# Attention and two MLPs on one core: q loaded in 256-byte runs without an on-chip copy, its scale with one operand, and another instruction order

## The chip, the cores and the metric

The kernel runs on one core of one Trainium2 chip. The metric is the device time of one execution in microseconds (us). TensorE multiplies matrices (PE in the views; PEld is its weight load), VectorE (DVE), ScalarE (ACT) and GpSimd (POOL) work element by element, and SyncE (SP) issues all DMAs from one queue, in order.

## What is computed

The reference, cut to what matters (B, H, S, D = 4, 8, 576, 64):

```python
scores = np.matmul(q, k.transpose(0, 1, 3, 2)) / np.sqrt(D)
scores = np.where((rel >= 0) & (rel < 128), scores - slope[h] * abs(rel), -1e9)   # rel = query - key
attn = np.exp(scores - scores.max(-1, keepdims=True))
attn = attn / (attn.sum(-1, keepdims=True) + 1e-9)
x = np.matmul(attn, v).transpose(0, 2, 1, 3).reshape(2304, 512)
h = x @ w_in                                                                      # 512 x 2048
g = (a[0] + a[1]*h + a[2]*h**2 + a[3]*h**3) / (1 + abs(b[0])*abs(h) + abs(b[1])*h**2 + 1e-6)
x = g @ w_out
g = np.maximum(x @ w2_in, 0) ** 2
return g @ w2_out
```

All data are float32 in memory.

## The kernel before

The attention takes its 32 heads as 16 pairs p (four pairs to a batch), the two heads of a pair on the two halves of the 128 partitions. The first 512 rows of a pair are four tiles of 128 queries; the last 64 rows of each batch are loaded and transposed on their own (`load_rem`, `tr_rem`). One pair goes through these steps:

- **Load.** `load_qk` issues two DMAs for q and two for k (one per head), `load_v` two for v. For pair 0, and for v always, row t*128+p of a head goes to partition p, so that each run of memory is one row of 64 numbers, 256 bytes. For q and k of pairs 1 to 15, rows 4p to 4p+3 go to partition p (L379): each run is 1 KB, in a tile `qw` or `kw` laid out head, row, column.
- **Mix** (plan steps `iq`, `ik`; pairs 1 to 15). `mix` copies such a tile into `qr` or `kr`, laid out row, head, column, so that a row of both heads lies together. POOL, ACT or DVE may do it.
- **Transpose** (`trq`, `trk`). `tr_main` transposes four 128x128 blocks on TensorE into one PSUM bank. Where rows were loaded four to a partition, the destination is strided by 4, which puts the columns back in order.
- **Copy** (`trqc`, `trkc`). `tr_copy` takes the bank to SBUF (`qkT`). For q it also multiplies by `qs`, one number per partition: ACT uses the function Identity with two operands that hold one number per partition, the scale `qs` and a bias tile `zero` of zeros (L433); DVE uses a multiplication (L435). k's copy is plain (L350 on ACT, L352 on DVE).
- **Scores and softmax.** `s_pe` (L449, L458) multiplies; on DVE `join_keys` (L473) and `ttr` (L483) add the bias and find the row minima of the negated scores; `exp` runs on ACT (L498); `pt_pe` transposes the exponentials on TensorE (L533, L538, L543); `pt_copy` takes them to SBUF as `ptsb` (two of five tiles on DVE at L553, the others a plain copy on ACT or DVE); `pv_pe` multiplies by v (L576 to L589); `x_copy` takes the result to SBUF as `xT`, and DMAs write it to DRAM. The sums' reciprocals go through TensorE (`r_tr`, L513), are copied as `rt` (`r_copy`), written to DRAM, and later multiplied into x.

Beside the pairs, the weights of the first MLP are loaded (512 KB a chunk, L207) and split into a high and a low half: `wb`, then `win1hi` (a plain rounding copy) and `win1lo` (a difference), on ACT, DVE and POOL. At about 140 us the matmuls of the MLPs begin (L836, L923, later L987), and from 160 us on there is nothing else on TensorE.

The order is made by the class `Plan`: each step is added with the engines that may do it and a cost on each, with the steps that it waits for, and a priority. `run` repeatedly picks the step and engine that can begin first by these costs, plus a correction from the table `HOLD` (by step kind and engine), ties broken by priority, to which the table `BIAS` adds a number by step kind. The result is a fixed program for each engine and for SP's queue; every engine runs its instructions strictly in that order. The tables hold 99 and 84 numbers.

What the change touches: `load_qk` (L362), `tr_main` (L409), `tr_copy` (L425), the tile `zero`, the plan entries of q's and k's loads, mixes, transposes and copies (L620 to L664), and both tables.

Of the kernel before, what the change touches and what calls it, by code (L numbers as in the profile page):

```python
# [1400 lines left out]
```

## Time and profile before

| | |
|---|---|
| median of 3 runs | 919.96 us (917.84 to 920.03) |
| the profiled execution's own time | 919.47 us |
| its span, first to last instruction | 917.7 us |
| TensorE busy | 897.5 us of the span |
| VectorE, ScalarE, GpSimd busy | 659.5, 523.9, 433.7 us |
| TensorE's granted clock, mean | 0.998 of full speed |
| read from and written to DRAM | 102.76 and 31.01 MB |

An engine's busy time is the union of its instructions; what is left of a stretch is idle time, in which it waited. The DMA share is the mean busy share of the core's 16 DMA engines. A matmul's end is modelled, so short waits can hide inside a busy TensorE. In the rows below the attention is cut at the starts of the L449 matmuls of pairs 4, 9 and 15 (49.12, 91.92 and 137.40 us), so the second stretch holds five pairs and the third six.

### The profile page before, as it was taken

How to read it: one execution, taken by the hardware profiler on the slowest of the kernel's cores; microseconds unless marked ns; L12 is line 12 of the kernel's file. 1: busy time of each engine (PE TensorE's matmuls, PEld its weight loads, DVE VectorE, ACT ScalarE, POOL GpSimd, SP SyncE). 2: the span in 40 equal slices, each digit the busy share in tenths (PEclk: the TensorE clock that was granted, in tenths of full speed). 3: DMA queues.
4: the chain of work that ended last, by engine and by line, in shares of the span. 5: the costliest groups of instructions: out<-in, count | busy, mean ns of one | idle time of the engine just before them, and what ended most of it. 6: DMA issues, size and time to landing. Idle time of an engine off the chain costs nothing.

```text
span 917.7 us, 14434 instructions
## 1 busy us (share of the span) xinstructions
PE 897.5 (98%) x4748; PEld 736.2 (80%) x4748; DVE 659.5 (72%) x1310; ACT 523.9 (57%) x1157; POOL 433.7 (47%) x457
## 2 busy tenths in 40 slices
PE   7988999999999999999999999999999999999998
PEld 6666666888998888888888888888888888888896
DVE  5999988988889887888789787876554534455422
ACT  4988887877788777767777763332322211121232
POOL 4476545777457777686858864421550200000100
PEclk9999999999999999999999999999999999999999
DMA  8799853321323542453252558554523634782010
GB/s 187 237 278 284 216 167 110 110 74 47 94 70 122 179 136 93 136 186 116 103 172 104 181 187 281 182 194 126 171 92 93 210 110 138 213 314 91 2 46 23
DMA packets 114443, 134.73 MB, mean 147 GB/s; under 512 B 37424, under 2 KB 76736, under 8 KB 114368
## 3 DMA queue, kind: packets, MB, share of 16 engines
q1 hardware_dynamic: 114368, 133.81, 46.8%
q8 instruction: 37, 0.61, 0.3%
q14 instruction: 38, 0.31, 0.1%
HBM read 102.76 MB, written 31.01 MB: 146 GB/s over the span
## 4 chain that ended last, share of the span: by engine, by line
PE 87%; ACT 4%; DVE 3%; DMA 2%; POOL 2%; issue 1%; SPq 0%; POOLq 0%; DVEq 0%
PE y L923 41%; PE h L836 23%; PE ps L987 16%; PE o L576 2%; PE s L458 2%; ACT e L498 2%; DMA xrraw<-ys 1%; PE warm L748 1%; PE tr L414 1%; PE pt L543 1%; DVE e L483 1%; DMA ys<-yt 1%; PE pt L533 1%; DMA kw<-in_k_dram 1%; ACT xT L350 1%
## 5 line engine op out<-in xcount | busy, mean ns | idle before, releaser
L987 PE MATMUL ps<-xh,wc 128*128 128x512 f32 x448 | 148.8, 389 | 0.3 <-ACT ah L350 0.3
L836 PE MATMUL h<-xh,win1hi 128*128 128x512 f32 (+1 forms) x320 | 118.1, 369 | 0.2 <-DVE gl L243 0.2
L923 PE MATMUL y<-gl,wout1hi 128*128 128x512 f32 (+1 forms) x320 | 117.7, 368 | 0.0
L836 PE MATMUL h<-xh,win1lo 128*128 128x512 f32 (+1 forms) x320 | 117.7, 368 | 0.0
L923 PE MATMUL y<-gh,wout1hi 128*128 128x512 f32 (+1 forms) x320 | 117.7, 368 | 0.0
L836 PE MATMUL h<-xl,win1hi 128*128 128x512 f32 (+1 forms) x320 | 117.7, 368 | 0.0
L923 PE MATMUL y<-gh,wout1lo 128*128 128x512 f32 (+1 forms) x320 | 117.7, 368 | 0.0
L865 POOL TENSOR_TENSOR t<-t,ah 128x512 f32<-128x512 f32 (+1 forms) x80 | 97.3, 1217 | 37.4 <-ACT t L860 31.6
L923 PE MATMUL y<-wout2hi,gh 128*128 128x512 f32 x288 | 112.1, 389 | 0.0
L923 PE MATMUL y<-wout2hi,gl 128*128 128x512 f32 x288 | 112.1, 389 | 0.0
L923 PE MATMUL y<-wout2lo,gh 128*128 128x512 f32 x288 | 112.0, 389 | 0.0
L236 ACT ACTIVATE gh<-ah 128x512 fp32r<-128x512 f32 x64 | 40.3, 629 | 109.8 <-DVE ah L1019 109.8
L987 PEld LDWEIGHTS ps<-xh,wc 128*128 128x128 f32 x448 | 84.1, 188 | 18.2 <-ACT ah L350 0.7
L987 PE MATMUL ps<-xl,wc 128*128 128x512 f32 x224 | 87.1, 389 | 0.0
L243 DVE TENSOR_TENSOR gl<-h,gh 128x512 fp32r<-128x512 f32 (+1 forms) x96 | 57.5, 599 | 39.3 <-ACT gh L236 38.3
L243 POOL TENSOR_TENSOR xl<-xr,xh 128x512 fp32r<-128x512 f32 (+1 forms) x18 | 20.1, 1128 | 129.6 <-ACT xh L236 129.3
L236 ACT ACTIVATE gh<-h 128x512 fp32r<-128x512 f32 (+1 forms) x96 | 50.3, 524 | 44.1 <-PE y L923 39.1
L243 DVE TENSOR_TENSOR gl<-ah,gh 128x512 fp32r<-128x512 f32 x64 | 49.3, 772 | 35.6 <-ACT gh L236 35.4
L836 PEld LDWEIGHTS h<-xh,win1hi 128*128 128x128 f32 x320 | 60.3, 188 | 10.7 <-DVE gl L243 0.6
L849 ACT ACTIVATE ah<-h 128x512 f32<-128x512 f32 (+1 forms) x80 | 44.2, 553 | 42.6 <-PE h L836 41.9
L923 PEld LDWEIGHTS y<-gh,wout1hi 128*128 128x128 f32 x320 | 60.4, 189 | 10.0
L836 PEld LDWEIGHTS h<-xl,win1hi 128*128 128x128 f32 x320 | 60.3, 189 | 10.0
(161 smaller groups left out, 2125.3 us busy)
## 6 DMA issues: line engine op xcount, KB each, us to landing
wc<-wsum SPq DMA_DIRECT2D x64, 256.0 KB, 3.9
wc<-wp SPq DMA_DIRECT2D x48, 256.0 KB, 3.6
win1r<-in_moe_w_in_dram SPq DMA_DIRECT2D x16, 512.0 KB, 5.1
wout1r<-in_moe_w_out_dram SPq DMA_DIRECT2D x16, 512.0 KB, 3.7
win2r<-in_moe_w_in_dram SPq DMA_DIRECT2D x16, 512.0 KB, 4.0
wout2r<-in_moe_w_out_dram SPq DMA_DIRECT2D x16, 512.0 KB, 4.7
xrraw<-ys SPq DMA_DIRECT2D x44, 128.0 KB, 4.0
xs<-xT SPq DMA_DIRECT2D x16, 288.0 KB, 4.5
```

The lines of the kernel that those rows point to most:

```text
L236: nc.scalar.activation(dst, src, AF.Copy)
L243: (nc.vector if eng == "DVE" else nc.gpsimd).tensor_tensor(dst, a, b, ALU.subtract)
L350: nc.scalar.activation(dst, src, AF.Copy)
L414: nc.tensor.transpose(dst, st[p]["qk"[n]][:, t].rearrange("p h d -> p (h d)"), ident)
L458: nc.tensor.matmul(ps[j][:, i % 2, :w], qT[js, qs_], kT[js, k0:k1], start=True, stop=True)
L498: nc.scalar.activation(e, e, AF.Exp, scale=-1.0, bias=s[:, j : j + 1], accum_out=sums[p % 3][:, c : c + 1],)
L576: nc.tensor.matmul(st[p]["o"][rows[j], kb * P : kb * P + w], vr[:, kb, j, :], pt[:, j, 2 * kb * P : 2 * kb * P + w], start=(i == 1), stop= ...
L836: nc.tensor.matmul(h[:, :n], a[:, c * P : (c + 1) * P], bb[:, :n], start=(m == 0), stop=(m == 3 * NCC - 1),)
L849: nc.scalar.activation(gt("ah", 2, ji, f), tl["h", ji, f], AF.Abs)
L865: nc.gpsimd.tensor_tensor(tl["t", ji, f], tl["t", ji, f], tl["ah", ji, f], ALU.mult)
L923: nc.tensor.matmul(dst, a, bb, start=(first and m == 0), stop=(last and m == 2))
L987: nc.tensor.matmul(dst, w, x, start=(k in (1, 2, 5) and m == 0), stop=(m == 5), skip_group_check=True)
```

## The change

Of q and k, only k (`LONG = 'k'`) keeps the 1 KB runs and the copy. q of every pair is loaded in 256-byte runs straight into `qr`, the tile that is transposed, and has no `qw` and no mix. Its load therefore waits for the transpose of q two pairs earlier (there are two `qr` tiles) and no longer for the mix two pairs earlier, and its transpose waits for the load itself. The number of DMAs stays; those of q have four times as many runs. On ACT, q's scale becomes the function Copy with the scale operand alone; `zero` goes. The costs of some steps are set anew, and both tables are replaced, so every engine's program is another. In the new program, ACT does all 17 scalings.

```diff
@@ the tables: 99 and 84 numbers replaced by 99 and 83
-BIAS = {'js': -354.3, 'm1': -417.1,
+BIAS = {'js': 653.6, 'm1': -2152.6,
...
@@ in the kernel
     MERGED = (2, 3)
+    LONG = 'k'
...
-    zero = acst.tile([P, 1], F32, name="zero")
...
-    nc.vector.memset(zero, 0.0)
...
         if t0 == 0:
-            if p == 0:
+            if p == 0 or nme not in LONG:
                 st[p][nme] = araw.tile([P, NQ - 1, 2, D], F32, tag=f"{nme}r", name=f"{nme}r{p}")
...
             rows = src[b, h0 + j, t0 * P : t1 * P, :]
-            if p == 0:
+            if p == 0 or nme not in LONG:
                 queue(eng).dma_start(st[p][nme][:, t0:t1, j, :], rows.rearrange("(t p) d -> p t d", p=P))
...
-            dst = ps[:, t * P : (t + 1) * P] if p == 0 else ps.rearrange("p (n t) -> p t n", t=NQ - 1)[:, t]
+            dst = ps[:, t * P : (t + 1) * P] if p == 0 or "qk"[n] not in LONG else ps.rearrange("p (n t) -> p t n", t=NQ - 1)[:, t]
...
-            nc.scalar.activation(dst, src, AF.Identity, bias=zero, scale=sc)
+            nc.scalar.activation(dst, src, AF.Copy, scale=sc)
...
-                    SP=1.15, move=(0.8 if p else 1.46) * w,
-                    after=[("i" + nme, p - 2), ("ld" + nme, p - 1)] + ([] if part else [("ldk0", p)]),
+                    SP=1.15, move=(0.8 if p and nme in LONG else 1.46) * w,
+                    after=[("i" + nme if nme in LONG else "tr" + nme, p - 2), ("ld" + nme, p - 1)] + ([] if part else [("ldk0", p)]),
...
-            if p:
+            if p and nme in LONG:
                 plan.add(
-                    ("i" + nme, p), lambda eng, p=p, nme=nme: mix(eng, p, nme), Pool=0.6, ACT=0.52, DVE=0.36,
+                    ("i" + nme, p), lambda eng, p=p, nme=nme: mix(eng, p, nme), Pool=0.69, ACT=0.53, DVE=0.6,
...
-                    PE=0.45 * w, after=[(f"i{nme}", p) if p else (f"ld{nme}{part}", p), last], prio=u0 - 5 + n,
+                    PE=0.45 * w, after=[(f"i{nme}", p) if p and nme in LONG else (f"ld{nme}{part}", p), last], prio=u0 - 5 + n,
...
-                    (tr + "c", p), lambda eng, p=p, n=n: tr_copy(eng, p, n), ACT=0.05 + 0.43 * w, DVE=0.06 + 0.54 * w,
+                    (tr + "c", p), lambda eng, p=p, n=n: tr_copy(eng, p, n), ACT=0.05 + 0.43 * w + 0.09 * (n == 0), DVE=0.06 + 0.54 * w + 0.06 * (n == 0),
```

Three places of the programs follow, before and now. A name's number is the pair (for `e` and `pt` the tile, five to a pair) or the weight chunk, with a tile number behind it; line numbers of the new kernel are one lower from L332 on.

SP's queue before, at the last load of q (pair 15); `rs8` is the write of pair 8's reciprocals:

```order
L389 DMA rem_3_1634<-in_q_dram 64x8x64
L389 DMA rem_3_1634<-in_k_dram 64x8x64
L389 DMA remv1_189<-in_v_dram 64x8x64
L379 DMA qw15_1661<-in_q_dram 128x256 x2
L603 DMA xs1_3_81<-xT7_1599 128x576
L379 DMA kw15_1690<-in_k_dram 128x256 x2
L401 DMA vr10_1705<-in_v_dram 128x4x64 x2
L207 DMA win1r_14_1734<-in_moe_w_in_dram 128x4x256
L522 DMA rs8_98<-rt8_1730 9x128
```

and now, from that write on:

```order
L521 DMA rs8_98<-rt8_1707 9x128
L207 DMA win1r_14_1726<-in_moe_w_in_dram 128x4x256
L602 DMA xs2_0_82<-xT8_1713 128x576
L376 DMA qr14_1750<-in_q_dram 128x4x64 x2
L400 DMA vr11_1773<-in_v_dram 128x4x64 x2
L378 DMA kw15_1798<-in_k_dram 128x256 x2
L521 DMA rs9_99<-rt9_1826 9x128
L207 DMA win1r_15_1844<-in_moe_w_in_dram 128x4x256
L602 DMA xs2_1_83<-xT9_1846 128x576
L376 DMA qr15_1878<-in_q_dram 128x4x64 x2
```

The last load of q stood ahead of the write of pair 8's reciprocals; now it comes after that of pair 9's, and after every chunk of `win1`.

DVE's program before, in pairs 6 and 7, with the mixes of pair 10:

```order
L238 COPY qr10_1197<-qw10_1108 128x2x4x64
L473 COPY_PREDICATED s6_1_1_1112<-after_c_160,s6_1_1_1112 128x2x128
L508 RECIPROCAL rc5_1117<-rc5_1117 128x9
L352 COPY ptsb6_1217<-pt30_1204 128x2x128
L483 ISA e32_1183,st32_1182<-s6_1_1_1112,rels_166 128x128
L483 ISA st32_1182 128x1
L238 COPY kr10_1226<-kw10_1088 128x2x4x64
L483 ISA e33_1188,st33_1187<-s6_1_1_1112,rels_166 128x128
L483 ISA st33_1187 128x1
```

and now, at the same mix of k:

```order
L243 TENSOR_TENSOR win1lo_8_1204<-wb8_1149,win1hi_8_1203 128x512
L552 TENSOR_TENSOR ptsb6_1212<-pt32_1227,halves_t_161 128x2x256
L552 TENSOR_TENSOR ptsb6_1212<-pt33_1231,halves_t_161 128x2x256
L482 ISA e35_1215,st35_1214<-s7_0_1_1178,rels_165 128x128
L482 ISA st35_1214 128x1
L238 COPY kr10_1260<-kw10_1118 128x2x4x64
L230 SCALAR_TENSOR_TENSOR win1r_9_1089<-win1r_9_1089 128x512
L482 ISA e36_1278,st36_1277<-s7_0_0_1177,rels_165 128x256
L482 ISA st36_1277 128x1
```

The mix of q (`qr10`) is gone from here, and so is the `ptsb6` copy.

ACT's program before, at the same `ptsb6` tiles (30 and 31):

```order
L498 ACTIVATE e32_1183,sums0_192<-e32_1183,st32_1182 128x128
L350 ACTIVATE qkT8_1136<-tr1_8_0_1210 128x512
L350 ACTIVATE ptsb6_1217<-pt31_1221 128x2x256
L498 ACTIVATE e32_1183,sums0_192<-e32_1183,st32_1182 128x128
L498 ACTIVATE e33_1188,sums0_192<-e33_1188,st33_1187 128x128 x2
L498 ACTIVATE e34_1193,sums0_192<-e34_1193,st34_1192 128x192
L498 ACTIVATE e35_1250,sums1_193<-e35_1250,st35_1249 128x128 x2
```

and now:

```order
L497 ACTIVATE e32_1115,sums0_190<-e32_1115,st32_1114 128x128
L497 ACTIVATE e33_1134,sums0_190<-e33_1134,st33_1133 128x128 x2
L349 ACTIVATE ptsb6_1212<-pt30_1198 128x2x128
L349 ACTIVATE ptsb6_1212<-pt31_1206 128x2x256
L349 ACTIVATE qkT8_1102<-tr1_8_0_1218 128x512
L497 ACTIVATE e34_1175,sums0_190<-e34_1175,st34_1174 128x192
```

ACT now makes both copies of pair 6's first two tiles; the copy of tile 30 came to it from DVE.

## Rows read from the trace of the kernel before

**Rows 1.** Windows view: length, each engine's busy us (instructions), PEclk, DMA share, GB/s.
```profile
12.50:49.10 36.60, 33.43 (x270) 22.61 (x268) 32.53 (x122) 32.39 (x114) 18.43 (x26) 0.95 0.85 237
49.10:91.90 42.80, 37.96 (x331) 26.17 (x330) 39.89 (x150) 36.32 (x138) 29.85 (x38) 1.00 0.98 275
91.90:137.40 45.50, 42.90 (x384) 28.96 (x383) 41.02 (x162) 39.84 (x154) 23.82 (x34) 1.00 0.68 192
137.40:160.00 22.60, 20.88 (x128) 15.75 (x129) 18.59 (x43) 16.55 (x43) 13.44 (x15) 1.00 0.30 103
160.00:917.70 757.70, 752.94 (x3589) 634.18 (x3588) 523.66 (x819) 396.92 (x712) 342.61 (x326) 1.00 0.41 133
```

**Rows 2.** TensorE's waits in 49.1 to 91.9 us: for whom, us in total, times, longest.
```profile
PE pt L538 <- DVE ptsb L553: 1.7, 2, 1.2
PE or L513 <- DVE ptsb L553: 0.8, 1, 0.8
```

**Rows 3.** The same view, 91.9 to 137.4 us.
```profile
PE o L576 <- ACT xT L350: 1.6, 2, 1.0
PE s L449 <- ACT qkT L350: 0.8, 2, 0.4
```

**Rows 4.** Groups by form, DVE, POOL: busy us, mean ns, idle before.
```profile
L352 DVE COPY ptsb<-pt 128x256 f32<-128x256 f32 x15 | 6.2, 415 | 1.6 <-PE pt L543 1.4
L352 DVE COPY ptsb<-pt 128x512 f32<-128x512 f32 x8 | 5.4, 674 | 2.2 <-PE pt L543 2.2
L238 DVE COPY kr<-kw 128x512 f32<-128x512 f32 x8 | 5.0, 622 | 1.9 <-DMA kw<-in_k_dram 1.9
L238 DVE COPY qr<-qw 128x512 f32<-128x512 f32 x4 | 2.5, 616 | 0.3 <-DMA qw<-in_q_dram 0.3
...
L240 POOL TENSOR_SCALAR qr<-qw 128x512 f32<-128x512 f32 x10 | 7.7, 771 | 2.8 <-PE tr L414 2.6
L240 POOL TENSOR_SCALAR kr<-kw 128x512 f32<-128x512 f32 x5 | 3.2, 650 | 10.3 <-DMA kw<-in_k_dram 6.1 <-PE tr L414 3.2 <-PE pt L543 0.9
```

**Rows 5.** The same view, ACT.
```profile
L433 ACT ACTIVATE qkT<-tr,zero,qs 128x512 f32<-128x512 f32 x15 | 11.5, 766 | 1.1 <-PE tr L414 0.9 <-ACT win1hi L236 0.2
L350 ACT ACTIVATE qkT<-tr 128x512 f32<-128x512 f32 x15 | 8.7, 577 | 1.0 <-PE tr L414 1.0
L350 ACT ACTIVATE ptsb<-pt 128x256 f32<-128x256 f32 x17 | 6.2, 365 | 1.0 <-PE pt L538 0.8 <-PE pt L543 0.3
L350 ACT ACTIVATE ptsb<-pt 128x512 f32<-128x512 f32 x8 | 4.6, 578 | 0.0
L350 ACT ACTIVATE rt<-or 9x128 f32<-9x128 f32 x16 | 4.1, 253 | 4.1 <-PE or L589 4.1
```

**Rows 6.** DMA view, 12 to 24 us: packets by size, then the queue's share.
```profile
DMA packets 5905, 2.52 MB, mean 210 GB/s; under 512 B 4448, under 2 KB 5904, under 8 KB 5904
q1 hardware_dynamic: 5904, 2.50, 95.2%
```

**Rows 7.** The same view, 24 to 32 us.
```profile
DMA packets 1862, 1.75 MB, mean 219 GB/s; under 512 B 160, under 2 KB 1861, under 8 KB 1861
q1 hardware_dynamic: 1861, 1.74, 69.0%
qw<-in_q_dram SPq DMA_DIRECT2D x2, 128.0 KB, 4.7
```

**Rows 8.** Timeline of SP's queue: start us, length, DMA issued.
```profile
22.71 0.90 SPq L379 DMA_DIRECT2D qw<-in_q_dram  x2
...
94.69 1.04 SPq L379 DMA_DIRECT2D qw<-in_q_dram  x2
```

**Rows 9.** Timeline of TensorE: q's transposes of pairs 3, 13 and 15.
```profile
30.39 0.60 PE L414 MATMUL tr<-ident,qr 128*128 128x128 f32 x4
...
105.81 0.60 PE L414 MATMUL tr<-ident,qr 128*128 128x128 f32 x4
...
120.91 0.60 PE L414 MATMUL tr<-ident,qr 128*128 128x128 f32 x4
```

More of the change, by code (lines that the diff above doesn't have):

```diff
@@ L105 @@
-HOLD = {('r_u', 'ACT'): 0.14, ('w0', 'DVE'): 3.0, ('xn', 'Pool'): -0.25, ('trq', 'PE'): 0.06, ('w5', 'Pool'): 0.1, ('r_t2', 'Pool'): 0.08, ('d4', 'DVE'): 2.89, ('w0', 'ACT'): 0.03, ('sl', 'Pool'): -0.57, ('g2', 'PE'): 0.27, ('trqc', 'DVE'): 2.07, ('xr', 'ACT'): -0.44, ('w1', 'DVE'): 2.9, ('r_p2', 'DVE'): 0.12, ('d2', 'Pool'): 0.47, ('d4', 'Pool'): 0.61, ('d2', 'DVE'): 2.07, ('xh', 'Pool'): 2.42, ('trk', 'PE'): 0.21, ('r_g1', 'DVE'): 0.06, ('rcp', 'DVE'): 0.09, ('xo', 'DVE'): 0.69, ('w0', 'Pool'): 0.03, ('pv', 'PE'): 0.07, ('trkc', 'DVE'): 1.86, ('w4', 'Pool'): 0.1, ('s', 'PE'): 0.12, ('w4', 'ACT'): 0.02, ('rtp', 'PE'): 0.17, ('trq0', 'PE'): 3.0, ('d3', 'DVE'): 3.0, ('wS', 'DVE'): 2.62, ('exp', 'ACT'): 0.02, ('js', 'DVE'): 0.08, ('trrc', 'ACT'): -0.36, ('sq', 'DVE'): -0.17, ('iq', 'DVE'): 0.03, ('g1', 'PE'): 0.01, ('d5', 'Pool'): -0.75, ('rtc', 'DVE'): 0.91, ('ptp', 'PE'): 0.04, ('c1', 'DVE'): 1.73, ('r3', 'DVE'): 1.51, ('scp', 'DVE'): 0.64, ('trk0c', 'ACT'): 2.37, ('ik', 'DVE'): -0.05, ('trq0c', 'ACT'): 1.37, ('rtc', 'ACT'): -0.11, ('c7', 'DVE'): -1.0, ('r_r1', 'ACT'): 0.09, ('trkc', 'ACT'): -0.01, ('w1', 'Pool'): -0.01, ('xl', 'DVE'): 0.06, ('ik', 'Pool'): -0.09, ('bias', 'Pool'): -0.18, ('iq', 'ACT'): 0.23, ('c6', 'ACT'): 0.79, ('c1', 'ACT'): 0.01, ('wS', 'Pool'): 0.03, ('r2', 'DVE'): 0.48, ('trq0c', 'DVE'): 0.3, ('ptc', 'ACT'): -0.03, ('c7', 'ACT'): 0.57, ('trr', 'PE'): -0.15, ('s_relu', 'ACT'): 0.24, ('r1', 'DVE'): 0.22, ('c4', 'ACT'): 0.76, ('m5', 'PE'): -0.13, ('xn', 'DVE'): 0.27, ('d5', 'DVE'): 0.35, ('m3', 'PE'): 1.04, ('m6', 'PE'): 0.02, ('d1', 'DVE'): 0.05, ('r_p1', 'DVE'): 0.01, ('warm', 'PE'): 0.4, ('d1', 'Pool'): 0.04, ('trk0', 'PE'): -0.13, ('m7', 'PE'): 0.06, ('m4', 'PE'): 0.59, ('yc', 'DVE'): 0.04, ('trk0c', 'DVE'): 0.03, ('c4', 'DVE'): 0.03, ('s_g', 'DVE'): 0.14, ('trrc', 'DVE'): -0.05}
@@ new lines @@
+HOLD = {('r_u', 'ACT'): 0.13, ('w0', 'DVE'): 3.0, ('xn', 'Pool'): -0.21, ('trq', 'PE'): 0.03, ('w5', 'Pool'): 0.15, ('w0', 'ACT'): 0.01, ('sl', 'Pool'): -0.82, ('g2', 'PE'): 0.59, ('trqc', 'DVE'): 2.81, ('xr', 'ACT'): -1.0, ('w1', 'DVE'): 2.73, ('r_p2', 'DVE'): 0.1, ('d2', 'Pool'): 0.57, ('d2', 'DVE'): 2.67, ('xh', 'Pool'): 2.29, ('r_g1', 'DVE'): 0.04, ('rcp', 'DVE'): 0.1, ('xo', 'DVE'): 2.2, ('w0', 'Pool'): 0.09, ('pv', 'PE'): 0.13, ('w4', 'Pool'): 0.11, ('rtp', 'PE'): 0.11, ('wS', 'DVE'): 1.75, ('js', 'DVE'): 0.08, ('trrc', 'ACT'): -0.28, ('r_r1', 'ACT'): 0.08, ('trkc', 'ACT'): -0.09, ('w1', 'Pool'): -0.01, ('xl', 'DVE'): 0.11, ('ik', 'Pool'): -0.09, ('iq', 'ACT'): 2.11, ('ptc', 'ACT'): -0.19, ('r_p1', 'DVE'): 0.08, ('d3', 'Pool'): 0.05, ('xh', 'ACT'): -0.05, ('gh', 'ACT'): -0.04, ('ik', 'ACT'): 2.54, ('iq', 'Pool'): 0.26, ('sh', 'ACT'): 2.87, ('d1', 'Pool'): 0.93, ('r_r2', 'ACT'): 0.06, ('s', 'PE'): 0.04, ('r_g3', 'DVE'): 0.01, ('iq', 'DVE'): 0.04, ('xl', 'Pool'): 0.1, ('trq0', 'PE'): 3.0, ('d5', 'Pool'): -0.51, ('d4', 'Pool'): 2.76, ('m2', 'PE'): 0.48, ('d1', 'DVE'): 2.41, ('g1', 'PE'): 0.26, ('d3', 'DVE'): 2.85, ('m4', 'PE'): 1.43, ('c1', 'ACT'): -0.68, ('xr', 'DVE'): 0.63, ('c4', 'DVE'): 1.65, ('wS', 'Pool'): 0.12, ('m7', 'PE'): 0.2, ('trq0c', 'ACT'): -1.0, ('trkc', 'DVE'): 3.0, ('s_relu', 'ACT'): 0.59, ('c4', 'ACT'): 0.07, ('c6', 'ACT'): 0.96, ('m5', 'PE'): -0.06, ('r3', 'DVE'): 1.2, ('trk', 'PE'): 0.05, ('r2', 'DVE'): -0.11, ('r1', 'DVE'): 0.17, ('c1', 'DVE'): -1.0, ('trrc', 'DVE'): 0.32, ('m1', 'PE'): 0.55, ('trk0c', 'ACT'): -0.26, ('sl', 'DVE'): 0.27, ('m3', 'PE'): 0.06, ('xn', 'DVE'): 0.18, ('plus', 'Pool'): -0.02, ('d5', 'DVE'): 1.57, ('c7', 'DVE'): 0.13, ('m6', 'PE'): -1.0, ('bias', 'Pool'): -0.19, ('trq0c', 'DVE'): -0.35, ('ptp', 'PE'): 0.01, ('trk0', 'PE'): 1.06}
```

2 lines of the change are left out of this document (1 added, 1 removed).

## The prediction

> **What bounds the kernel now.** I read the windows view first [rows 1]. From 160 us to the end TensorE is busy for 752.94 of 757.70 us. The change leaves that work alone, so it can only win time before 160 us. There TensorE's idle time, length less busy time, is 3.17, 4.84, 2.60 and 1.72 us in the four stretches, together 12.3 us: the ceiling of any gain. The 12.5 us ahead of them are start-up, which I leave as it is. The granted clock is 1.00 from 49.1 us on, the level of 2.4 GHz.
>
> The second stretch is the worst. TensorE idles for 11.3% of it (4.84 of 42.80), with DVE busy for 93% (39.89) and a DMA share of 0.98. In the third it idles for 5.7% (2.60 of 45.50), with DVE at 90% and DMA at 0.68. The waits tell the two apart: in the second the two longest of TensorE end with copies of `ptsb` on DVE, 1.7 and 0.8 us [rows 2]; in the third all that are named end with ACT, 1.6 and 0.8 us [rows 3]. So in the middle of the attention DVE is late, perhaps with the DMAs beside it, and after that ACT's copies are. Short waits also hide in the modelled ends: a matmul takes 37.96/331 = 114.7 ns of busy time in the second stretch and 42.90/384 = 111.7 ns in the third, on nearly the same mix of work. Over 331 matmuls that is 1.0 us.
>
> **The change part by part.** The sum is made against the profiled execution's own 919.47 us, of which 1.77 us lie outside its span; the median of the runs is 0.49 us above it.
>
> *Mixes of q, and who does the other copies.* Fifteen mixes go, ten from POOL (771 ns each) and four from DVE (616 ns) [rows 4], one from ACT. Counting both programs, seven wide and nine half-wide copies of `ptsb` move from DVE (674 and 415 ns [rows 4]) to ACT (578 and 365 ns [rows 5]); eleven copies `rt` move from ACT (253 ns) to DVE, where I price them the same; four mixes of k leave DVE (622 ns) and two ACT, and POOL gets those six (650 ns); four roundings `win1hi` go from ACT (priced as a plain copy, 577 ns) to POOL; pair 0's scaling and copy, half-wide, go from DVE to ACT (415 ns each). Sums:
>
> - DVE: -4.7 - 3.7 - 2.5 - 2.5 - 0.8 + 2.8 = -11.4 us
> - ACT: +4.0 + 3.3 - 1.7 - 2.8 - 2.3 + 0.8 = +1.3 us, before the scale
> - POOL: -7.7 + 3.9 + 2.6 = -1.2 us
>
> Single moves of other weight instructions, of both signs, I leave out.
>
> *q's scale.* No row has Copy with one operand per lane. With two it takes 766 ns, with none 577 [rows 5]; these are the bounds. Taking half of the difference for each operand gives 672 ns, so ACT gets 15 x 0.094 = 1.4 us back, and its sum is -0.1 us. The multiplication by `qs` itself stays.
>
> *What DVE's relief is worth.* 11.4 us over 16 pairs is 0.71 us a pair, 3.6 us for the five pairs of the second stretch. DVE's share there falls from 93% to 85%, below the 90% that it has in the third, and the mixes of k and q no longer stand ahead of its `ptsb` copies. I take it that TensorE's idle share falls to that of the third stretch: 42.80 x (11.3% - 5.7%) = 2.4 us. Of the 1.0 us of hidden waits I take half. That makes **-2.9 us**, with ends at 0 (ACT's copies are late in DVE's place) and -5.8 us (all of the 4.84 and the 1.0). For the other three stretches I take 0: the named waits of the third are on ACT, whose work does not change. The bounds are half the third's idle time, 1.3 us either way, and -1.1 us for the first (3.17 us down to 5.7% of 36.60).
>
> *q's DMAs.* Their number and bytes stay, their runs are four times as many. Two windows give the prices: in 12 to 24 us, 4448 packets under 512 B and 1456 of about 1 KB took 95.2% of 16 engines, 182.8 us [rows 6]; in 24 to 32 us, 160 and 1701 took 69.0%, 88.3 us [rows 7]. Solved for both, a small packet costs 24.9 ns and a 1 KB one 49.6 ns. One pair's q goes from 256 x 49.6 to 1024 x 24.9 ns, over 16 engines from 0.79 to 1.59 us: +0.80 us a pair, +12.0 us over 15 pairs. The ends are 0 (only bytes count) and +1.49 us a pair (every packet of the first window costs 182.8/5904 = 31 ns; 768 more a pair). The idle DMA time in the first three stretches is 5.5, 0.9 and 14.6 us, so there is room in all but the second.
>
> The Trainium skill's page "DMA: Bandwidth & Descriptors", section "Specifications", speaks against this part: it asks for transfers of at least 512 B to reach line rate. The trace agrees, at 10.3 bytes per ns against 20.6. Its section "Why small descriptors are slow (HBM only)" counts 11 cycles for 256 B of which 8 carry data; an estimate from it is 44 cycles against 35 for 1 KB, +3 us in all; the trace's factor of two decides.
>
> I put the cost on the path at 0, because q is loaded well ahead. Before, pair 15's load was issued at 94.69 us [rows 8] and transposed at 120.91 [rows 9], 26 us later. Now it can go out only after the transpose of pair 13, at 105.81 before: 15.1 us ahead, of which landing takes 4.7 [rows 7]. 10 us remain. In SP's queue v, the next k and a weight chunk stand behind that new wait; k's loads also run pairs ahead. The tight place is early: pair 3's load left at 22.71 us for a transpose at 30.39, and its place in the queue has not moved. Three loads of q cost 2.4 us more by then; 7.7 - 4.7 - 2.4 leaves 0.6 us, and the mix (0.6 to 0.8 us) that lay between is gone. If that cover fails, TensorE pays up to 2.4 us.
>
> *The rest.* The transposes are as many and as long. Some steps after 160 us are dealt out anew, U copies among them; TensorE idles there for 4.76 us, mostly at the very end, so a new order can hardly win. I take 0, bounds 0 and +3.
>
> Sum: 919.47 - 2.9 = **916.6 us**, 3.4 us (0.37%) under the median before.
>
> **The rivals.**
>
> *ACT takes DVE's place: 919.5 us.* For it: ACT is busy for 85% of the second stretch and 88% of the third [rows 1], it receives 16 `ptsb` copies (+7.3 us), and the roundings and mixes taken from it lie elsewhere. TensorE would wait for `ptsb` as before, only for ACT. If Copy with one operand costs no less than Identity did, ACT has 1.4 us more still. Against it: its sum is flat, and its copy is 50 to 96 ns shorter than DVE's. Time: no relief, 919.5.
>
> *The DMAs become the bound: 922.6 to 926.6 us, slower.* In the second stretch DMA is at 0.98 already; five pairs of q add 5 x 0.80 = 4.0 us, less 0.9 of room: +3.1 us without any relief. If the first stretch cannot use its gaps either, its five loads add as much as 4.0 us. It decides from where q's loads land after their transposes' turn: at pair 3, with 7.7 - 4.7 = 3.0 us to spare over three loads, from +1.0 us a pair, against the 0.80 that I solved for and the upper end of 1.49. For it: k's mixes waited for their DMA before, 6.1 us on POOL and 1.9 on DVE [rows 4]. Against it: the later pairs' lead and the 14.6 us of idle DMA behind. The skill's rule of 512 B, cited above, points this way.
>
> *More is gained: 913.3 us.* The new order could halve all 12.3 us of idle time, as 15 mixes fewer free POOL and every hand-over.
>
> *The later stages lose it: 919.6 us or more.* A new order after 160 us that stalls TensorE for 3 us eats the gain. Little speaks for it: the largest share of that time has an idle TensorE of under 1%.
>
> **How the numbers follow.** About 0.3%, 2.8 us, is what a measurement of this kernel tells from no change: faster is below 917.2, slower above 922.7. Chances: my forecast 0.42, with a spread of 915 to 918.2 of which 0.30 lies below 917.2; more gained 0.15; ACT in DVE's place 0.22; the DMAs 0.15, nearly all of it slower; the later stages 0.06, mostly slower when it also loses the relief. Faster is 0.30 + 0.15 = 0.45; slower 0.14 + 0.05 = 0.19; the same 0.36. The range is 912.5 to 923.0: it takes in the larger gain and the DMA case's lower edge, and leaves out that case's upper part.
>
> **What would show it.** Right: between the L449 matmuls of pairs 4 and 9, DVE at about 85%, TensorE's idle share near 6%, no long wait of TensorE for `ptsb` on DVE; q's scale at about 672 ns; the DMA share at 0.95 or more until some 105 us and higher behind it than 0.68; no wait of TensorE that ends with q's DMA. Wrong: transposes of q that wait for their DMA, k's mixes waiting longer than before, ACT above 92% with `ptsb` late, or idle TensorE after 160 us above 5 us.

## The result, and the profile after

The changed kernel takes 911.15 us (median of 6 runs, 910.26 to 912.76), the kernel before 919.61 beside it on the same chip. The ratio is 0.9910 with a 95% interval of 0.9894 to 0.9926: faster by 8.5 us. The forecast had the sign, but 916.6 us is 5.5 us too slow, and 911.15 lies below the range (912.5 to 923.0).

The profiled execution took 911.93 us, its span 910.2 us, 7.5 us less than before (the medians differ by 8.5; no row tells where the last 1 us lies). The windows view, cut as in [rows 1] at the scores' matmuls (now L448) of pairs 4, 9 and 15, and then where the same work is left on TensorE as at 160 us before (3590 groups, 3589 before):

```profile
12.50:49.27 36.77, 33.01 (x269) 22.16 (x265) 30.49 (x126) 32.37 (x116) 17.78 (x26) 0.95 0.87 237
49.27:88.08 38.81, 37.56 (x334) 25.88 (x331) 38.05 (x141) 34.74 (x131) 24.88 (x34) 1.00 1.02 286
88.08:131.46 43.38, 42.91 (x384) 29.20 (x384) 38.60 (x164) 41.64 (x159) 24.84 (x36) 1.00 0.77 216
131.46:153.26 21.80, 20.48 (x126) 15.33 (x126) 17.52 (x35) 17.86 (x42) 10.57 (x13) 1.00 0.31 110
153.26:910.20 756.94, 752.52 (x3590) 634.43 (x3589) 523.02 (x828) 403.22 (x714) 324.68 (x316) 1.00 0.41 133
```

Against [rows 1] the stretches change by +0.17, -3.99, -2.12, -0.80 and -0.76 us, together -7.5. TensorE's idle time in the second falls from 4.84 to 1.25 us, in the third from 2.60 to 0.47. And yet DVE is busy for 98% of the second stretch (93% before) and ACT for 96% of the third (88%).

TensorE's waits, in the second stretch and then in the third, where only one is left:

```profile
PE s L457 <- DVE st L482: 0.7, 1, 0.7
PE pt L537 <- ACT qkT L349: 0.4, 1, 0.4
...
PE pt L537 <- DVE ptsb L552: 0.2, 1, 0.2
```

The waits for `ptsb` of [rows 2] (1.7 and 0.8 us) and those for ACT of [rows 3] (1.6 and 0.8 us) are gone. The groups by form that answer to [rows 4, 5]:

```profile
L432 ACT ACTIVATE qkT<-tr,qs 128x512 f32<-128x512 f32 x15 | 10.2, 683 | 0.8 <-PE tr L413 0.6
L349 ACT ACTIVATE ptsb<-pt 128x256 f32<-128x256 f32 x26 | 9.9, 381 | 1.0 <-PE pt L537 0.6 <-PE pt L542 0.2
L349 ACT ACTIVATE ptsb<-pt 128x512 f32<-128x512 f32 x15 | 9.0, 598 | 1.6 <-PE pt L542 1.3
L240 POOL TENSOR_SCALAR kr<-kw 128x512 f32<-128x512 f32 x11 | 7.3, 660 | 7.5 <-DMA kw<-in_k_dram 7.2 <-DMA vr<-in_v_dram 0.2
L351 DVE COPY rt<-or 9x128 f32<-9x128 f32 x11 | 3.1, 278 | 2.9 <-PE or L588 1.8 <-ACT qkT L349 0.7 <-ACT ptsb L349 0.2
L238 DVE COPY kr<-kw 128x512 f32<-128x512 f32 x4 | 2.2, 552 | 0.2 <-DMA kw<-in_k_dram 0.2
```

q's scale takes 683 ns where it took 766. DVE's 23 plain copies of `ptsb` have become 7, ACT's 25 have become 41, and POOL makes most copies of k.

### The profile page after: what moved, and what is told of

It reads as the page before. It is cut to its first block, busy times and chain, and to the rows that moved or that the text cites. A ratio compares the mean times of both kernels' runs of the same rounds, so it can differ in the third digit from the quotient of the medians.

```text
span 910.2 us, 14425 instructions
## 1 busy us (share of the span) xinstructions
PE 896.0 (98%) x4748; PEld 735.7 (81%) x4748; DVE 650.6 (71%) x1305; ACT 532.7 (59%) x1162; POOL 408.5 (45%) x441
## 4 chain that ended last, share of the span: by engine, by line
PE 85%; ACT 0%; DMA 0%; DVE 0%; issue 0%; SPq 0%
PE y L922 43%; PE h L835 24%; PE ps L986 17%; PE o L575 0%; DMA xs<-xT 0%; PE s L457 0%; PE pt L542 0%; PE pt L532 0%; PE pt L537 0%; DVE ptsb L552 0%; ACT ptsb L349 0%; ACT yt L349 0%; ACT xT L349 0%; ACT e L497 0%; PE s L448 0%
## 5 line engine op out<-in xcount | busy, mean ns | idle before, releaser
L922 PEld LDWEIGHTS y<-gh,wout1lo 128*128 128x128 f32 x320 | 60.4, 189 | 10.0
L835 PEld LDWEIGHTS h<-xh,win1lo 128*128 128x128 f32 x320 | 60.3, 188 | 10.0
```

Source lines behind the costliest of these rows:

```text
L835: nc.tensor.matmul(h[:, :n], a[:, c * P : (c + 1) * P], bb[:, :n], start=(m == 0), stop=(m == 3 * NCC - 1),)
L922: nc.tensor.matmul(dst, a, bb, start=(first and m == 0), stop=(last and m == 2))
```

## The experiments

Each kernel was run beside the kernel before on the same chip. To compare between groups I use the ratio to it; a difference of 0.001 is 0.9 us. The expectations, which subtract medians, have 2.9 us for e1 and 3.8 for e3 where the ratios give 2.7 and 3.5. Letters of theories hold within one group of experiments only.

### One part undone, everything else in the changed kernel's order

**e1**: the scale with two operands again.

```diff
-            nc.scalar.activation(dst, src, AF.Copy, scale=sc)
+            nc.scalar.activation(dst, src, AF.Identity, bias=zero, scale=sc)
```

> The changed kernel in its own order, only q's scale on ScalarE again with two operands by lane (Identity with a bias of zeros). The changed kernel itself took 911.15 us against 919.61 before, a ratio of 0.991. Theory A (the gain comes from work taken off VectorE, and ScalarE, now the busiest of the three from pair 9 on, can take little more): the scale goes from 683 to about 766 ns, 15 times, 1.2 us of ScalarE, and 0.3 to 1.2 us of it is seen: 911.5 to 912.4. Theory B (the shorter scale is a main part of the gain): 913 or more. Theory C (the order alone counts): 911.2.

Measured: 914.08 us (912.32 to 914.33), ratio 0.9939 (0.9927 to 0.9952), 2.7 us above the change, in theory B's range and above A's. Fifteen times 83 ns are 1.2 us on ACT; the path pays more than twice that. The second stretch is 40.49 us, 1.7 longer, with ACT busy for 36.28 of it: there ACT is not full, and I take the added time to go through hand-overs.

**e2**: q in 1 KB runs, not put in order.

```diff
+                    flat = st[p][nme].rearrange("p t h d -> p (t h d)").rearrange("p (j t d) -> p j t d", j=2, d=D)
+                    queue(eng).dma_start(flat[:, j], rows.rearrange("(p t) d -> p t d", p=P))
```

> The changed kernel in its own order, q loaded in 1 KB runs again but without the copy: left out is the putting in order of q's rows, so the scores are of other rows; the instructions and their number stay, and 12 us of DMA time go. Theory A (q's 256-byte runs are hidden, as its loads run ahead): 910.5 to 911.8. Rival D (the DMAs, at a share of 1.02 in the middle stretch, pace the middle of the attention): 908 to 909.5, with the gain between pairs 4 and 9.

Measured: 910.73 us (910.01 to 911.98), ratio 0.9908 (0.9895 to 0.9922): the same as the change, as theory A has it. In this order the 256-byte runs cost nothing on the path.

**e3**: 26 plain `ptsb` copies back on the engines of before.

```diff
+        eng = "DVE" if u in [5, 9, 16, 19, 20, 21, 25, 26, 30, 39, 40, 45, 46, 51, 59, 60, 64, 66, 70, 71, 76] else "ACT" if u in [24, 36, 54, 74, 75] else eng
```

> The changed kernel in its own order, but each ptsb copy on the engine that made it before: 21 go from ScalarE back to VectorE, 5 from VectorE to ScalarE. VectorE gets about 8 us more, ScalarE 7 us less. Theory A (VectorE's relief is the gain): TensorE waits for ptsb again, 913 to 916. Theory C (who copies is of no account as long as the order of the steps is the new one): 911 to 912.

Measured: 914.99 us (913.86 to 915.36), ratio 0.9948 (0.9935 to 0.9962), 3.5 us above the change, in theory A's range. Its windows of the second and third stretch:

```profile
49.60:89.91 40.31, 37.88 (x334) 25.77 (x330) 39.68 (x148) 33.31 (x127) 25.96 (x33) 1.00 0.97 273
89.91:135.12 45.21, 42.93 (x386) 29.37 (x385) 41.70 (x173) 39.48 (x152) 24.06 (x36) 1.00 0.74 208
```

They lose 1.5 and 1.8 us; DVE has 1.6 and 3.1 us more to do.

**e4, e5**: q in 1 KB runs and its 15 mixes, one pair ahead of the transposes, all on DVE (e4) or on GpSimd (e5).

```diff
+        if p and "qw" in st.get(p + 1, ()) and "q" not in st[p + 1]:
+            mix("DVE", p + 1, "q")
```

> The changed kernel in its own order, with q in 1 KB runs and its copy back, all 15 on VectorE, one pair ahead of the transpose: 15 times 0.6 us, 9.3 us more on VectorE, 12 us less of DMA time. Theory A: 913 to 916, with VectorE near 95% between pairs 4 and 9. Theory C: 911 to 912. Rival D (DMA paces the middle): below 911.

> As e4 (the changed kernel in its own order, q in 1 KB runs with its copy back, 12 us less of DMA time), but all 15 copies on GpSimd, which is busy for only 64% of the middle stretch. With the copies on VectorE the kernel took 916.35 us, 5.2 above the changed one. Theory A (what counts is VectorE, which is at 98% there, and ScalarE): GpSimd has room, 911 to 913.5. Rival E (any work put back delays a hand-over somewhere in the strict order, whichever engine does it): 915 or more.

Measured: e4 916.35 us (914.34 to 918.51), ratio 0.9967 (0.9956 to 0.9979), 5.2 us above the change; e5 913.22 us (912.43 to 916.30), 0.9947 (0.9926 to 0.9967), 3.4 us above, between 0 and 7 by the ends of both intervals. e4 lies just above theory A's range; e5 lies in A's by its median, and between A's and rival E's by its ratio. So in this order every part but the runs' length is worth 3 to 5 us when it is taken back by itself; for the mixes that holds for the place in the programs that I gave them by hand. They cannot be added: e1, e3 and e4 together would make 11.4 us of the 8.5.

### One part done, in the order of before

**e6**: q direct, its mixes left out, with two more tiles for it (tag `ah`), so that a load waits for the transposes of four pairs earlier.

```diff
+            if nme == "q" and p % 2:
+                raw = gp.tile([P, T], F32, tag="ah", name=f"qr{p}", bufs=2)
+                st[p][nme] = raw.rearrange("p (t h d) -> p t h d", h=2, d=D)
...
+        if nme == "q":
+            return
```

> The kernel before in its own order, only that q is loaded in 256-byte runs straight into the tile that is transposed (four such tiles, so that the loads keep their places in the queue) and the 15 copies go. DMA gets 12 us more in the stretch where its share is 0.98, and earlier than in the changed kernel. Theory A: four copies leave VectorE (2.5 us) and ten GpSimd: 1 to 3 us under the kernel before, 916.5 to 918.5. Rival D (here the DMAs are in the way, which the new order avoided by loading q later): 920 or more. Rival E: 914 or less.

**e10**: the scale's line alone. **e11**: e6 and e10 together.

```diff
-            nc.scalar.activation(dst, src, AF.Identity, bias=zero, scale=sc)
+            nc.scalar.activation(dst, src, AF.Copy, scale=sc)
```

> The kernel before in its own order, only q's scale with one operand by lane. In the changed kernel's order the same edit was worth 2.9 us (e1), for 1.2 us of ScalarE's work. Theory A1 (the scale lies in a chain of transpose, copy, next transpose, scores, in every pair): 1.5 to 3 us under before, 916 to 918. Rival F (in the old order VectorE ends the waits, so ScalarE's gain is not seen before pair 9): 0 to 1 us, 918.2 to 919.3.

> e6 and e10 together: the kernel before in its own order with q loaded directly and the scale with one operand. What is missing to the changed kernel (911.15) is then the new order, with the ptsb copies that it deals to ScalarE. Theory A: about 915 to 917, so that the new order and its sharing out of the copies are worth 4 to 6 us. Theory G (the parts do it, whatever the order): 911 to 912.5. Theory C (the order does it all): 918.5 to 920.

Measured: e6 920.68 us (917.45 to 921.82), ratio 1.0014 (1.0000 to 1.0027); e10 918.86 us (916.94 to 922.12), 1.0002 (0.9990 to 1.0015); e11 919.75 us (916.70 to 920.58), 1.0010 (1.0000 to 1.0020). Nothing is gained, although all the work that the edits remove is gone. By their medians e6 lies in rival D's range, e10 in rival F's and e11 in theory C's. The two waits of [rows 2], 1.7 and 0.8 us before, are still there in e11's second stretch (47.10 to 92.16 us; its lines are five higher):

```profile
PE pt L543 <- DVE ptsb L558: 1.6, 2, 1.1
...
PE or L518 <- DVE ptsb L558: 1.1, 1, 1.1
```

DVE's groups by form in the same stretch show one place where the relief went:

```profile
L238 DVE COPY kr<-kw 128x512 f32<-128x512 f32 x6 | 5.9, 977 | 2.2 <-DMA kw<-in_k_dram 2.2
L230 DVE SCALAR_TENSOR_TENSOR win1r<-win1r 128x512 int32<-128x512 int32 x6 | 5.0, 831 | 0.8 <-POOL win1r L225 0.8
```

In the same view of the kernel before, the six `kr` took 3.9 us (651 ns each), the six `win1r` 4.5, and the two `qr` that e11 saves 1.6 us. So 1.6 us went and 2.5 us came, in instructions that nobody had touched. The timeline of e11 shows why:

```profile
47.80 1.27 POOL L243 TENSOR_TENSOR win1lo<-wb,win1hi 128x512 fp32r<-128x512 f32 x1 [0.65 <-ACT win1hi L236]
47.91 1.44 DVE L238 COPY kr<-kw 128x512 f32<-128x512 f32 x1 [1.13 <-DMA kw<-in_k_dram]
...
68.22 1.29 POOL L243 TENSOR_TENSOR xl<-xr,xh 128x512 fp32r<-128x512 f32 x1
68.28 1.51 DVE L238 COPY kr<-kw 128x512 f32<-128x512 f32 x1
```

and those of the kernel before (the copy that is at 47.91 in e11) and of e4 show it begun while GpSimd is at rest:

```profile
49.45 0.43 DVE L238 COPY kr<-kw 128x512 f32<-128x512 f32 x1 [0.65 <-DMA kw<-in_k_dram]
...
28.05 0.42 DVE L238 COPY kr<-kw 128x512 f32<-128x512 f32 x1
```

Both slow copies began just after an instruction of GpSimd (at 47.80 and 68.22) and ended 0.28 us after it: 49.35 against 49.07, 69.79 against 69.51. The copy that takes 0.42 us alone waits, "busy" by the profile, until GpSimd is done. Both of these instructions of GpSimd were there before; DVE's copies have moved. The first comes later than before, since it waited 1.13 us for its DMA and not 0.65, and falls on a `win1lo` that it had been ahead of (49.45 against 49.81); the second comes earlier, since the mix of q that ran ahead of it at 67.73 is gone, and meets all of an `xl` (before, it began at 69.27, 0.34 us before the end of the `xl`). In e6, which has the same q, the six copies average 744 ns: small shifts decide.

Whether q's short runs also cost something in this order, as rival D says, stays open. In e6's first two stretches the DMA share is 0.99 and 1.04 (before 0.85 and 0.98), but no wait of TensorE of over 0.2 us ends there with a DMA, and the waits of all engines for DMAs add up to 7.6 us, before 11.4. No run in the order of before leaves the mixes out and keeps the 1 KB runs.

### Is it the order, or who does which copy?

The two plans differ, before 160 us, in the engine of 71 operations: 26 `ptsb`, 11 `rt` and 6 `kr` copies, and 28 others, mostly of the weights. e13 is e11 with these 71 on the changed kernel's engines, e14 the changed kernel with them on the engines of before, e15 the kernel before with nothing but them moved.

```diff
+            eng = SHARE.get(name, eng)
             fn(eng) if len(engs) > 1 else fn()
```

> The order of before, q loaded directly and the scale with one operand, and 71 operations that are planned before 160 us (26 ptsb copies, 11 rt copies, 6 kr copies, parts of the gate's and the weights' splitting) on the engines that they have in the changed kernel. Theory A, the gain is the sharing-out of the copies among ACT, DVE and GpSimd, in whatever order: 911 to 913 us. Theory B, the gain is the new order itself, and the sharing only belongs to it: 918 to 921, as with the old sharing (919.75). Theory C, sharing and order fit each other and each gives a part: 914 to 917.

> The changed kernel in its own order, but the same 71 operations on the engines that they have before the change. A: all of the gain goes, 918 to 921 us. B: little goes, 911 to 913. C: 914 to 917; moving the 26 ptsb copies alone cost 3.8 us (914.99), so under A most of what is left, 4 us, hangs on the 45 others, and under B and C they add under 1 us.

> The kernel before with the same 71 operations on the engines that they have in the changed kernel; q is still put in order by 15 copies and the scale still takes two operands. A: most of the gain without any of the edits, 912 to 916 us (the copies of q on DVE and GpSimd cost 2 to 5 us in the new order). B: 918 to 921. If q's copies in the old order fill what the sharing frees on DVE: 917 to 919.

Measured: e13 922.92 us (922.42 to 924.25), ratio 1.0047 (1.0034 to 1.0060); e14 918.81 us (917.60 to 919.41), 0.9994 (0.9986 to 1.0003); e15 925.05 us (923.22 to 927.15), 1.0063 (1.0049 to 1.0077). A falls by e13, B by e14. e13 and e15 lie above every range that I had given them. C named the right cause and a wrong size: order and sharing do not give a part each. With the edits, the order alone gives nothing (e14) and the sharing alone costs 4 us (e13); together they give 8.5. The windows of the second and third stretch, of e14:

```profile
49.02:90.42 41.40, 37.88 (x334) 26.11 (x330) 39.03 (x148) 33.39 (x128) 25.40 (x32) 1.00 0.96 268
90.42:136.55 46.13, 43.48 (x386) 29.26 (x385) 41.52 (x167) 42.13 (x162) 22.17 (x32) 1.00 0.74 203
```

and of the third stretch of e13:

```profile
91.81:139.64 47.83, 43.79 (x383) 29.12 (x382) 37.75 (x158) 40.02 (x152) 24.77 (x36) 1.00 0.72 192
```

And in that stretch of e13 the waits of TensorE, DVE and ACT:

```profile
PE pt L541 <- ACT e L506: 1.4, 3, 0.8
...
DVE ptsb L561 <- PE pt L541: 4.0, 4, 1.7
...
DVE rt L355 <- ACT qkT L353: 1.4, 3, 0.7
...
ACT qkT L353 <- PE or L597: 2.1, 4, 0.8
```

In e13 no engine is full: TensorE idles for 4.04 us, DVE is at 79%, ACT at 84%. TensorE waits for ACT, ACT and DVE for TensorE, DVE for ACT. I read this as steps that stand at the wrong place of an engine's fixed program and hold up all behind them; which steps they are was not tried one by one.

### Are the tables enough?

**e16**: the kernel before with only the two tables exchanged. **e7**: the changed kernel with q in 1 KB runs and mixed, planned anew. **e8**: the changed kernel with the old tables. **e9**: the changed kernel with k direct too, planned anew.

```diff
-    LONG = 'k'
+    LONG = 'qk'
```

(e7; in e9 `LONG = ''`.)

> The kernel before with nothing but the two tables of numbers exchanged for those of the change, so that the planner orders and shares out the old code (q put in order, scale with two operands, the old costs) anew. Theory D, the tables are the gain whatever the code: 911 to 914 us. Theory E, the edits make it possible, and the tables alone give an order as good as the old one or worse: 917 to 923.

> The changed kernel with q loaded in 1 KB runs and put in order by 15 copies again, planned by the new tables and the new costs; the scale keeps one operand. D: 911 to 914 us. E: 915 to 921; the same copies put back into the changed kernel's fixed order gave 913.2 on GpSimd and 916.4 on DVE, so a planner that may move everything should do no worse than 916 if its plan is worth anything.

> The changed kernel with the old tables: q direct, scale with one operand, the new costs, everything planned anew. If the edits are the gain once engines and order are chosen together: 911 to 915 us. If the search over the tables is needed too (D or both): 916 to 922.

> The changed kernel with k loaded directly too, the order found by its own rules from the same tables. It takes 15 kr copies off (11 on GpSimd of 660 ns, 4 on DVE of 552) and adds about 0.8 us of DMA a pair, 12 us in all, where the DMA engines show a share of 1.02 in pairs 4 to 9. If the DMA engines are the next bound: 4 to 5 us more in that stretch, 913 to 917 us. If the DMA share there is cover for other waiting, and DVE with its share of 98% the bound: DVE loses 2.2 us, 908 to 911. If the tables fit only the code they were found for, the order worsens: 916 to 922.

Measured: e16 932.91 us (931.53 to 935.01), ratio 1.0142 (1.0119 to 1.0166); e7 928.44 us (927.07 to 931.77), 1.0102 (1.0083 to 1.0122); e8 933.48 us (932.74 to 935.29), 1.0156 (1.0135 to 1.0177); e9 917.62 us (916.44 to 918.22), 0.9984 (0.9976 to 0.9993). D falls; E has the sign, but e16, e7 and e8 lie 7 to 12 us above its ranges. In these three a table taken over from other code costs 9 to 14 us; in e9, which falls in its third range (916 to 922), the new tables keep 1.5 of the 8.5 us. In e16 and e7 about 9 us of the loss lie behind the attention, in work that nothing but the tables touches: the last window, some 757 us long in both kernels, is 767.0 us in both (3583 and 3591 groups of TensorE's work), of which TensorE is busy for 754.3 and 755.8. From 165 us on its longest wait in e16 is 3.0 us, for `U` on DVE; before it is 0.3 us. Within the attention the new tables do gain with each edit: pair 15's scores begin at 143.3 us in e16, at 136.5 in e7 (new costs, one operand), and at 131.5 in the changed kernel (q direct), against 137.4 before, each from one execution.

### What bounds the changed kernel?

**e17**: the changed kernel's own order, k loaded directly into the tiles that held its 1 KB runs, its 15 mixes left out.

```diff
     def mix(eng, p, nme):
+        return
```

> The changed kernel in its own order and sharing, with k loaded directly as well into the tiles that held its 1 KB runs, and its 15 copies left out (11 of 660 ns on GpSimd, 4 of 552 ns on DVE). If DVE and the engines behind it are the bound: 2 us less, 908 to 910.5. If the DMA engines become it (12 us more of DMA time, share 1.02 in pairs 4 to 9): 912 to 916. If the extra DMA time is covered and the freed time on DVE is not where the end is set: 910.5 to 912, as the changed kernel.

Measured: 924.58 us (921.55 to 926.83), ratio 1.0049 (1.0029 to 1.0069), outside all three expectations. Its second stretch is 46.92 us, 8.1 longer than the changed kernel's, and the DMA share in it falls from 1.02 to 0.87: in e17 the DMA engines get less to do, they do not hold the others up. Part of the 8.1 us is TensorE's clock: after TensorE had idled for 1.87 us, the granted clock fell to 0.50 (1.2 GHz) between 69 and 71 us, and TensorE is busy for 2.0 us longer in the stretch (39.57 against 37.56). The waits of SP's queue there:

```profile
SPq L376 <- PE pt L533: 7.5, 3, 3.7
SPq L376 <- PE tr L414: 3.7, 2, 2.3
```

The longest wait of a load (L376) in the changed kernel's second stretch is for another DMA:

```profile
SPq L376 <- DMA win1r<-in_moe_w_in_dram: 1.8, 2, 1.1
```

The mix had emptied the load's tile early. Without it the tile comes free only after the transposes, the next load of k waits for that at the head of SP's queue, and every DMA behind it waits too. The timeline of e17 has such a load of k right behind the transposes of k:

```profile
51.09 0.60 PE L414 MATMUL tr<-ident,kw 128*128 128x128 f32 x4
51.72 0.92 SPq L376 DMA_DIRECT2D kw<-in_k_dram  x2
```

For q the change has the same dependence, but the planner knew of it and put q's loads later (pair 15: 104.53 us, before 94.69 [rows 8]).

**e18**: DVE's 4 `kr` copies on GpSimd. **e19**: 3 `win1lo` and one `xl` of pairs 5 to 9 on GpSimd.

```diff
+SHARE = {('ik', 3): 'Pool', ('ik', 4): 'Pool', ('ik', 7): 'Pool', ('ik', 10): 'Pool'}
```

(e18; in e19 `w5` of chunks 8, 10 and 11, and `xl` of tile 1.)

> The changed kernel with DVE's 4 kr copies (pairs 3, 4, 7 and 10, mean 552 ns) on GpSimd, all else in place. If DVE's share of 98% is the bound there: up to 2.2 us less, 909 to 910.5. If GpSimd beside DVE slows DVE's own work as much as it takes off, or the order is what sets the time: 910.5 to 913.

> The changed kernel with 3 win1lo and one xl of pairs 5 to 9 on GpSimd, where the kernel before has them. On DVE they take 1029 and 1112 ns there, on GpSimd 1278. If DVE is the bound: up to 4.2 us less, 907 to 910. If GpSimd's later end makes the weights' chain late, or the engines slow each other: 911 to 914.

Measured: e18 911.77 us (909.81 to 913.56), ratio 0.9926 (0.9910 to 0.9941), not to be told from the change; e19 914.83 us (913.07 to 916.17), 0.9959 (0.9943 to 0.9975), 4.5 us slower and above both of its ranges, although DVE's share in the second stretch (47.69 to 89.18 us) falls to 89% (36.88 of 41.49 us). How much of this the moved work costs is not shown: the granted clock in that stretch of the profiled execution is 0.96, and TensorE is busy there for 1.8 us longer than in the changed kernel. In e9 DVE is at 78% in the second stretch (31.55 of 40.41 us), which is 1.6 us longer than in the changed kernel. So a lower DVE share made no kernel faster than the changed one; nothing here shows the 98% to be the bound, and giving DVE's work to GpSimd did not help. Of the kernels tried that do the whole work, none beats the change.

## Why the prediction was right and wrong

**Where time could be won: right.** It came from the stretches before 160 us, 6.7 of 7.5 us; the rest is 0.76 us behind, forecast as 0 with bounds 0 and +3, and outside them.

**The relief in the second stretch: the right waits, near in size, wrong in its cause.** Forecast -2.9 us with ends at 0 and -5.8; measured -4.0: TensorE's idle time fell by 3.6 (forecast 2.4) and its busy time by 0.4 (hidden waits, forecast 0.5). The waits for `ptsb` on DVE went, as forecast. But the copies' move did not do it alone: in e13, with the same moves and both edits in the old order, this stretch takes 42.61 us against 42.80 before, and in e3, with the moves taken back in the new order, 1.5 us of the 4.0 are lost. That -2.9 came close is partly luck.

**"For the other three stretches I take 0": this step failed.** The third gave -2.1 us (bounds 1.3 either way) and the fourth -0.8; with the last and the first, 3.5 of the 7.5 us lie in what I had put at 0. It rested on "the named waits of the third are on ACT, whose work does not change". ACT's work there rose (39.84 to 41.64 us), and the waits went all the same. So they did not hang on how much ACT had to do. They hung on the order and the sharing together: that stretch is 47.83 us long in e13 and 46.13 in e14, against 45.50 before and 43.38 now.

**Load taken for time: the error behind it.** I priced moved work, turned a lower busy share into fewer waits, and put the new order at nothing. DVE was to fall to 85%; it rose to 98%. Its busy time fell by 1.8 us in that stretch, not 3.6, since two `win1lo` more and an `xl` ran on DVE there (left out as "single moves of other weight instructions", of both signs) and waits for GpSimd count as busy (those `win1lo` take 1029 ns each, 676 before). e11, e13 and e14 show it from the other side: the same relief in the old order gives nothing, the same sharing-out there costs 4 us, and the new order with the old sharing gives nothing.

**The scale: price right, value wrong.** Forecast 672 ns, measured 683. On the path I took 0 for it. That is right for the old order (e10: 1.0002) and wrong for the new one (e1: 2.7 us).

**q's DMAs: 0 on the path, right; the price too high.** e2 shows the 0. No wait of TensorE ends with q's DMA, though the lead shrank: pair 15's load goes out at 104.53 us for a transpose at 114.56, 10.0 us (forecast 15.1). The DMA view of the changed kernel, 12 to 24 us and 24 to 32 us, to be read as [rows 6, 7]:

```profile
DMA packets 7077, 2.73 MB, mean 227 GB/s; under 512 B 5732, under 2 KB 7076, under 8 KB 7076
q1 hardware_dynamic: 7076, 2.71, 88.4%
...
DMA packets 3203, 1.58 MB, mean 197 GB/s; under 512 B 2188, under 2 KB 3201, under 8 KB 3201
q1 hardware_dynamic: 3201, 1.56, 70.0%
```

Solved as before, a 1 KB packet costs 49.6 ns as it did, a small one 18.0, not 24.9. From 12 to 160 us the queue's packets take 76.9% of the DMA engines' time, in e2 74.8%: 0.021 x 148 = 3.1 us for q's short runs, where I had 12.0. The estimate of 3 us that I drew from the Trainium skill's page "DMA: Bandwidth & Descriptors", section "Why small descriptors are slow (HBM only)", and set aside agrees with this. In the old order, though, e6 takes 81.6% against 74.8% before, 10.1 us: the same short runs have no one price, and what sets it was not tried.

**The rivals.** "More is gained" (913.3 us, chance 0.15) was nearest. I tied it to freed time on POOL, and POOL was not the point. ACT in DVE's place did not happen: ACT passed the 92% that I had named (96% in the third stretch), but `ptsb` was not late. The DMAs did not become the bound, and k's mixes waited for theirs no longer than before (7.4 us against 8.0). That the edits could be worth nothing without a new order was no case of mine.

**What stays open.** Whether a new search of the tables for the old code would have found as good an order was not tried; e16, e7 and e8 show only that a table taken over from other code is worth nothing. Nor were both edits taken back at once in the new order, so what that order and its sharing give without them is not known. So how much of the 8.5 us belongs to the edits and how much to the search can't be said. What is shown is that the edits without the new order and sharing give nothing, and that with them each is worth 3 to 5 us when it is taken back (that of q's copies on GpSimd with a wide interval). Which steps of the new order do it is not shown.

## What to carry to other kernels

Where every engine runs a fixed program, the worth of an edit is a matter of the order it lands in: try it in the old order first, and if it gives nothing there, ask what the order waits for before giving it up. Where all engines wait for each other in turn, a busy share tells neither the bound nor the gain; look at single instructions and what ran beside them. Before removing a copy, ask whose tile it sets free: here the same removal was worth 3 to 5 us for q, where the order had been made for it, and cost 13 for k, where it had not.

## What the hardware showed that I had not expected

- **DVE and GpSimd shut each other out.** A copy from SBUF to SBUF on DVE takes 0.42 us alone and 1.44 or 1.51 beside GpSimd, and ends 0.28 us after GpSimd's instruction in both cases, not at some slower rate. It goes the other way too: before, a mix of q on GpSimd took 0.61 us at 81.81 and 1.04 us at 90.33, where it began during an instruction of DVE (L230, 90.20 to 90.89) and ended 0.48 us after it. A copy out of PSUM was not held up: e11's `ptsb` copy on DVE at 67.73 took 0.43 us with GpSimd busy from 66.99 to 68.28. My price of 622 ns for `kr` was a mean over both. The Trainium skill's page "SBUF — State Buffer", section "SBUF: two separate sides", says that GpSimd and some of DVE's operations share one pair of ports, which is locked for a whole instruction, so that the other is blocked rather than slowed; these ends agree. I had not drawn on it.
- **Taking work away can lengthen what is left.** e11's `kr` copies on DVE went from 651 to 977 ns in the second stretch, because two of them slid onto instructions of GpSimd.
- **A small packet has no fixed price:** 24.9 ns before, 18.0 ns after, solved from the same two windows with one price for each size.
